# Sparse attention followed by a dense layer: strided loads held behind two DMA transposes, transposes re-ordered, the instruction order dealt anew

## The chip, the cores and the metric

One NeuronCore of a Trainium2 chip runs the whole program. The metric is the device time of one execution in microseconds (us), lower is better. Its engines are TensorE (PE in the profile, PEld for its weight loads), VectorE (DVE), ScalarE (ACT), GpSimd (POOL) and SyncE (SP). Here POOL issues all loads, which turn float32 into bfloat16 on the way, and SP issues all stores of the output and all DMA transposes. Each engine works through its own instructions in the order in which the program gives them.

## The reference

Eight batches of eight heads, 576 positions, head size 64. Heads 0 to 3 attend locally (the last 32 positions), heads 4 to 7 with a stride (positions that are a multiple of 32 back). The result, 4608 tokens of 512 features, goes through a dense layer with an ELU between two matrices.

```python
B, H, S, D = q.shape            # 8, 8, 576, 64
scores = scale * np.matmul(q, k.transpose(0, 1, 3, 2))
rel = pos[:, None] - pos[None, :]
mask_local = (rel >= 0) & (rel < stride)                       # heads 0 to 3
mask_strided = (rel >= 0) & (pos[None, :] % stride == pos[:, None] % stride)   # 4 to 7
attn = softmax(where(mask, scores, -1e9))
x = (attn @ v).transpose(0, 2, 1, 3).reshape(B * S, H * D)     # 4608 x 512
h = x @ w_in                                                   # 512 -> 2048
g = np.where(h > 0.0, h, np.exp(np.minimum(h, 0.0)) - 1.0)
out = g @ w_out                                                # 2048 -> 512, float32
```

## The kernel before

Attention is done batch by batch and the dense layer chunk by chunk, 512 tokens to a chunk, nine chunks. A batch has 576 tokens, so chunk 4 (tokens 2048 to 2559) needs batches 3 and 4, chunk 5 batches 4 and 5, chunk 6 batches 5 and 6. The normalised result of attention is kept transposed in `xT` (features on partitions), the form that the dense layer's matmuls read.

What each engine does, and when, is written out by hand in one list of tokens, `ORDER`. The program goes through it and records the instructions of each token; the queue of each engine is therefore the tokens of that engine in this order, and a token's place among tokens of other engines matters only for what it can depend on. The tokens:

- `4s0.tq@2` and the like belong to attention: batch 4, kind s (strided) or l (local), pair of heads 0 or 1; the number after @ is the PSUM bank, the letter after / the engine (A for ACT, D for DVE, S for a DMA transpose from SP). The steps of a pair: `tq`, `tk`, `cq`, `ck` transpose q and k on TensorE and copy them (batches 0 to 2 only); `S` scores; `e`, `F0`, `F1` the exponentials on ACT; `m0`, `M` the masks on DVE; `v0`, `v1`, `halo` bring v into place; `a` is probabilities times v; `n` normalises into `x_sb` on DVE (the profile's x_s and x_l, L661 and L663).
- Then x has to be transposed into `xT`. Early batches do it on TensorE (`x`, L671) with a copy `y`. From batch 4 on it is done by DMA. For local heads `y/S` is one DMA transpose from SP (L685) straight into `xT`. For strided heads `z` is a DMA transpose from SP (L679) into a part of the tile `qT_str` of that batch, which is free by then, and `y` is a copy by DVE or ACT from there into `xT` (L700, L702).
- `i4.0@2` is hidden tile 0 (of 16) of chunk 4: four matmuls over the four feature blocks (L739), in `C_ORDER`, which takes the strided heads first: 4s0's block, 4s1's, then the local ones. `x4.0@2` is its Exp on ACT (L744). `r4.0` and `g4.0` finish the ELU: `r/D` is L750 on DVE, `r/A` a Relu on ACT (L748), `g` is L759 or L756 on DVE.
- `o4.1.2` is a quarter of the sixteen output matmuls of 128 tokens (L765); `c4.1/A` copies the result out of PSUM (L772) and issues its store from SP (L780). The three buffers `o_sb` are used in turn.
- `load.6` issues all loads of batch 6 from POOL: local q, k, v (L299, L303, L287), then strided q, k, v (L275, L279), each strided tensor as five DMAs. At most eight of POOL's DMAs are under way at a time: each issue waits for the landing of the one eight before it. The same holds for SP's DMAs.
- From batch 3 on, q and k are transposed by DMA: `turn.6s` (L309, two DMA transposes, q then k) and `turn.6l` (L315, four), from SP. Each waits for its loads, and all that follows on SP waits with it.

In the list of before, the queue of SP has between chunks 1 and 5 this order (`c` is a store): `turn.4s turn.4l c1.3 c2.0 turn.5s c2.1 turn.5l 4l0.y c2.2 4l1.y 4s0.z 4s1.z c2.3 turn.6l c3.0 c3.1 turn.6s 5s0.z 5l0.y c3.2 5l1.y 5s1.z c3.3 turn.7l c4.0 turn.7s c4.1 6l0.y 6l1.y c4.2 6s0.z 6s1.z`. POOL has `load.2` to `load.7` one after the other.

Of the kernel before, what the change touches and what calls it, by code (L numbers as in the profile page):

```python
# [11 lines left out]
BF16 = mybir.dt.bfloat16  # L12
# [39 lines left out]
0l0.tq@2 0s1.n@1 0l1.tq@3 0l0.cq/A 0s0.x@4 0l1.cq/A 0l0.s1@0 0s0.y/D load.2 0l1.s0@1  # L52
0l0.e1 0l0.halo/D 0s1.x@2 0l1.e0 0l1.s1@0 0s1.y/D 0l0.s0@1 0l1.e1 0l1.halo/D 0l0.e0
mk.l busy.2 0l1.a@0 0l0.a@1 0l1.n@0 0l0.n@1 busy.2 0l1.x@3 i0.0.0@4 0l1.y/A i0.2.0@2
i0.0.1 0l0.x@0 i0.1.0@3 i0.1.1 0l0.y/D i0.2.1 i0.0.2 i0.0.3 i0.1.2 i0.1.3 x0.0@0
i0.2.2 i0.2.3 x0.1@1 i0.3@5 r0.0/D x0.2@2 g0.0 r0.2/D r0.1/A x0.3@0 g0.1 r0.3/D i0.4@4
# [18 lines left out]
r1.10/A x1.12@2 g1.10 r1.11/A r1.12/D i1.14@2 x1.13@1 g1.11 g1.12 r1.13/A i1.15@5
load.4 x1.14@0 g1.13 o1.0.0@3 r1.14/A x1.15@2 g1.14 o1.0.1 r1.15/D g1.15 2l0.S@0,1,4,2
o1.0.2 2l0.e o1.1.0@5 2l0.F0 2l0.m0 2l0.F1 2l1.e o1.0.3 2l0.M 2l0.a@0 2l1.m0 3s0.v0/A
turn.3s o1.1.1 2l0.n@0 3s0.v1/A 2l1.a@1 c1.0/A o1.1.2 3s1.halo/D 2l1.n@1 2l0.x@4
o1.1.3 turn.3l 2l0.y/D 2l1.x@2 o1.2.0@3 c1.1/A 2l1.y/D i2.0@4 i2.1@5 x2.0@1 i2.2@2
r2.0/D x2.1@0 g2.0 o1.2.1 r2.1/A x2.2@2 g2.1 i2.3@4 r2.2/D i2.4@5 g2.2 x2.3@1 i2.5@2  # L80
r2.3/D x2.4@0 g2.3 o1.2.2 r2.4/A x2.5@2 g2.4 i2.6@4 r2.5/D i2.7@5 g2.5 x2.6@1 i2.8@2
r2.6/D x2.7@0 g2.6 load.5 o1.2.3 r2.7/A x2.8@2 g2.7 i2.9@4 r2.8/D c1.2/A g2.8
3s0.S@0,1,5,3 x2.9@1 i2.10@2 r2.9/D 3s0.e g2.9 3s0.F0 i2.11@4 3s0.m0 3s0.F1 3s1.e
3s0.M 3s0.a@0 x2.10@0 i2.12@5 3s1.m0 x2.11@2 3s0.n@0 turn.4s 3s1.a@1 r2.10/A o1.3.0@3
r2.11/A 3s1.n@1 x2.12@1 3s0.x@0 o1.3.1 3s0.y/A g2.10 3s1.x@1 r2.12/A g2.11 turn.4l
i2.13@2 3s1.y/A g2.12 i2.14@4 x2.13@0 o1.3.2 r2.13/D x2.14@2 g2.13 i2.15@5 r2.14/A
g2.14 o1.3.3 x2.15@1 3l0.S@0,1,2,4 r2.15/D c1.3/A g2.15 o2.0.0@3 3l0.e o2.0.1 3l0.F0
3l0.m0 3l0.F1 3l1.e 3l0.M o2.0.2 3l1.m0 3l0.a@0 o2.0.3 3l0.n@0 3l1.a@1 c2.0/A 3l0.x@5
3l1.n@1 o2.1.0@2 3l0.y/A 3l1.x@4 o2.1.1 3l1.y/D i3.0@3 i3.1@5 x3.0@0 4s0.v0/D i3.2@4
r3.0/D x3.1@2 g3.0 o2.1.2 r3.1/A 4s0.v1/D x3.2@1 g3.1 load.6 i3.3@3 r3.2/D i3.4@5 g3.2  # L90
x3.3@0 turn.5s i3.5@4 r3.3/D x3.4@2 g3.3 o2.1.3 r3.4/A x3.5@1 g3.4 i3.6@3 r3.5/D
c2.1/A g3.5 4l0.S@0,1,5,2 turn.5l x3.6@0 i3.7@4 r3.6/D 4l0.e g3.6 4l0.F0 i3.8@3 4l0.m0
4l0.F1 4l1.e 4l0.M o2.2.0@5 x3.7@2 4l1.m0 i3.9@2 x3.8@1 r3.7/D g3.7 r3.8/A o2.2.1
x3.9@0 g3.8 i3.10@4 r3.9/D g3.9 4s1.halo/A o2.2.2 x3.10@2 4l0.a@0 r3.10/D 4l1.a@1
4l0.n@0 i3.11@3 o2.2.3 4l1.n@1 4l0.y/S x3.11@1 i3.12@2 r3.11/A g3.10 c2.2/A g3.11
x3.12@0 4s0.S@0,1,4,5 4l1.y/S r3.12/D i3.13@3 g3.12 4s0.F0 4s0.F1 4s0.e o2.3.0@4 4s0.M
4s1.e o2.3.1 4s0.m0 x3.13@2 4s0.a@0 4s1.m0 i3.14@5 4s0.n@0 r3.13/A 4s1.a@1 x3.14@1
o2.3.2 4s1.n@1 4s0.z r3.14/A i3.15@2 g3.13 o2.3.3 g3.14 x3.15@0 4s1.z o3.0.0@3 r3.15/D
c2.3/A g3.15 5l0.S@0,1,5,4 o3.0.1 5l1.e o3.0.2 5l0.e 5l1.m0 turn.6l o3.1.0@2 5l0.F0
5l0.m0 5l0.F1 o3.0.3 5l0.M o3.1.1 c3.0/A o3.1.2 4s0.y/A o3.1.3 5s0.v0/D 5s0.S@0,1,5,4  # L100
c3.1/A 4s1.y/D o3.2.0@3 5s0.e 5s0.v1/D turn.6s load.7 i4.0@2 5s0.F0 5s0.m0 5s0.F1
5s1.e i4.1@5 5s0.M x4.0@2 i4.2@4 5s1.m0 x4.1@1 r4.0/D o3.2.1 g4.0 r4.1/A x4.2@0 g4.1
i4.3@2 r4.2/D i4.4@5 g4.2 x4.3@2 i4.5@4 r4.3/D x4.4@1 g4.3 5s0.a@0 r4.4/A i4.6@2
x4.5@0 g4.4 o3.2.2 r4.5/D x4.6@2 g4.5 i4.7@5 r4.6/A 5s0.n@0 5s1.halo/A i4.8@4 g4.6
5s0.z x4.7@1 5l0.a@1 x4.8@0 5l1.a@0 5l0.n@0 i4.9@2 r4.7/A r4.8/A o3.2.3 5l1.n@1
5l0.y/S x4.9@2 5s1.a@1 r4.9/A g4.7 c3.2/A g4.8 i4.10@5 5l1.y/S g4.9 i4.11@3 5s1.n@1
x4.10@1 i4.12@4 r4.10/A x4.11@0 5s1.z g4.10 o3.3.0@2 x4.12@2 r4.11/D i4.13@5 g4.11
r4.12/A g4.12 o3.3.1 x4.13@1 5s0.y/D o3.3.2 r4.13/A g4.13 i4.15@3 o3.3.3 x4.15@0
o4.0.0@4 r4.15/D c3.3/A g4.15 i4.14@5 6l0.S@0,1,2,3 x4.14@2 o4.0.1 r4.14/D 6l0.e g4.14
o4.0.2 6l0.F0 5s1.y/D 6l0.F1 6l1.e o4.0.3 6l0.m0 turn.7l i5.0@5 6l0.M c4.0/A 6l1.m0  # L110
# [44 lines left out]
def kernel(  # L155
# [9 lines left out]
    nc = tc.nc  # L165
# [837 lines left out]
```

## Time and profile before

| | us |
|---|---|
| median of three runs (lowest to highest) | 317.56 (315.15 to 317.68) |
| the profiled execution | 316.84 |
| its span, first to last instruction | 315.0 |
| TensorE busy in it | 299.4 (95%) |
| DVE busy | 216.3 (69%) |
| ACT busy | 194.1 (62%) |

Lines of the profile are read so. In the window view a line is a stretch (from:to, its length), then the busy time and number of instructions of PE, PEld, DVE, ACT and POOL, then the granted TensorE clock (1.00 is full), the mean busy share of the 16 DMA engines, and GB/s. In the timeline a line is the start, the duration (merged over xN instructions), the engine (SPq for what SP's queue issues), the line of the kernel, and in brackets the idle time of the engine before it and what ended that. In the page's groups a line ends with busy time, mean ns of one, and the idle time before. For a DMA, the duration in the timeline is that of its issue; the time to landing stands in views of its own.

### The profile page before, as it was taken

To read this page: it belongs to the slowest core of one execution; us is meant where nothing else is said; L and a number is where in the kernel's file an instruction comes from. 1 tells how busy PE (TensorE), PEld (TensorE's weight loads), DVE (VectorE), ACT (ScalarE), POOL (GpSimd) and SP (SyncE) were. 2 spreads that over 40 slices of the span, in tenths; PEclk is the share of its full clock that TensorE was granted. 3 is DMA by queue.
4 is the path that set the end of the run, shared out by engine and by line. 5 is a ranking of instruction groups with operands and counts; after the bars stand their busy time and mean duration, and the time that the engine had idled before them with its cause. 6 is when DMAs were issued, how large, how long until landed. Compare 5 with 4: busy or idle time off the path is not lost.

```text
span 315.0 us, 6035 instructions
## 1 busy us (share of the span) xinstructions
PE 299.4 (95%) x2227; PEld 156.8 (50%) x2264; DVE 216.3 (69%) x425; ACT 194.1 (62%) x353; POOL 127.5 (40%) x200
## 2 busy tenths in 40 slices
PE   8989999999999999999799999999999999999992
PEld 3644555655554554554345454544554454444440
DVE  4769734799768876896279687985896486666400
ACT  8748636799557856875569586556667554443210
POOL 8845337797694786766356742000000000000000
PEclk9999999999999999999989999999999999999998
DMA  6999999999999999999999999920033301112012
GB/s 102 141 204 210 210 153 212 125 109 100 138 154 161 134 184 151 116 179 152 144 124 186 166 147 150 194 67 33 33 74 75 67 2 34 33 39 66 33 69 73
DMA packets 113348, 37.35 MB, mean 119 GB/s; under 512 B 95848, under 2 KB 107760, under 8 KB 113312
## 3 DMA queue, kind: packets, MB, share of 16 engines
q0 software_dynamic: 71232, 18.41, 69.8%
q1 hardware_dynamic: 42080, 18.49, 34.8%
q8 instruction: 19, 0.31, 0.5%
q14 instruction: 17, 0.14, 0.2%
HBM read 36.70 MB, written 9.44 MB: 146 GB/s over the span
## 4 chain that ended last, share of the span: by engine, by line
PE 77%; DVE 12%; DMA 4%; issue 2%; ACT 2%; POOL 0%; ACTq 0%; DVEq 0%
PE single L765 35%; PE single L739 32%; DMA qT_str<-x_s 3%; DVE g_sb L759 3%; PE pair L651 3%; DVE g_sb L756 2%; DVE g_sb L750 2%; PE single L405 2%; PE pair L558 2%; DVE x_s L663 1%; DVE x_l L663 1%; DMA q_loc<-in_q_dram 1%; PE single L671 1%; ACT pr L636 1%; DVE rden L661 1%
## 5 line engine op out<-in xcount | busy, mean ns | idle before, releaser
L739 PE MATMUL single<-xT,w_in 128*128 128x512 bf16 x559 | 139.3, 383 | 4.8 <-ACT o_sb L772 2.0
L765 PE MATMUL single<-w_out_sb,g_sb 128*128 128x512 bf16 x558 | 136.5, 379 | 1.7 <-issue 0.8
L744 ACT ACTIVATE e_sb<-single 128x512 f32<-128x512 f32 x144 | 86.0, 602 | 66.6 <-PE single L739 63.0
L739 PEld LDWEIGHTS <-w_in 128*128 128x128 bf16 x576 | 64.0, 114 | 61.9 <-issue 7.7
L765 PEld LDWEIGHTS <-g_sb 128*128 128x128 bf16 x576 | 54.4, 98 | 61.8 <-issue 0.5
L750 DVE TENSOR_SCALAR g_sb<-e_sb 128x512 bf16<-128x512 f32 x89 | 40.8, 458 | 38.2 <-ACT e_sb L744 37.9
L759 DVE TENSOR_TENSOR g_sb<-g_sb,single 128x512 bf16<-128x512 bf16 x89 | 61.0, 687 | 3.1
L756 DVE SCALAR_TENSOR_TENSOR g_sb<-e_sb,g_sb 128x512 bf16<-128x512 f32 x55 | 37.1, 688 | 2.4 <-ACT g_sb L748 2.3
L636 ACT ACTIVATE pr<-pair 128x960 bf16<-128x960 f32 (+4 forms) x36 | 32.0, 900 | 7.2 <-PE single L558 4.1
L772 ACT COPY o_sb<-single 128x512 f32<-128x512 f32 x31 | 18.2, 586 | 26.1 <-PE single L765 25.9
L748 ACT ACTIVATE g_sb<-single 128x512 bf16<-128x512 f32 x55 | 32.6, 600 | 0.0
L651 PEld LDWEIGHTS <-pr 128*128 128x128 bf16 (+3 forms) x364 | 15.1, 102 | 5.8 <-DVE pr L611 0.6
L299 POOL DMA_DIRECT2D q_loc<-in_q_dram x20 | 15.3, 794 | 4.6 <-DMA k_str<-in_k_dram 2.7
L299 POOL DMA_DIRECT2D k_loc<-in_k_dram x20 | 15.0, 762 | 3.9 <-DMA v_raw<-in_v_dram 2.1
L663 DVE TENSOR_TENSOR x_l<-pair,rden 96x768 bf16<-96x768 f32 x16 | 15.3, 954 | 0.6
L663 DVE TENSOR_TENSOR x_s<-pair,rden 126x640 bf16<-126x640 f32 (+1 forms) x16 | 14.0, 874 | 0.5
L269 POOL DMA_DIRECT2D v_raw<-in_v_dram x18 | 10.7, 602 | 7.2 <-DMA w_out_sb<-in_moe_w_out_dram 4.8
L275 POOL DMA_DIRECT2D q_str<-in_q_dram x20 | 12.7, 646 | 1.1 <-DMA k_loc<-in_k_dram 1.0
L275 POOL DMA_DIRECT2D k_str<-in_k_dram x20 | 12.2, 621 | 2.0 <-DMA q_str<-in_q_dram 1.4
L275 POOL DMA_DIRECT2D v_raw<-in_v_dram x20 | 12.2, 626 | 1.6 <-DMA k_str<-in_k_dram 0.9
L661 DVE RECIPROCAL rden<-pair 96x12 f32<-96x12 f32 (+4 forms) x48 | 7.8, 189 | 6.8 <-PE pair L651 3.4
L287 POOL DMA_DIRECT2D v_loc<-in_v_dram x9 | 10.8, 1198 | 3.3 <-DMA q_str<-in_q_dram 1.2
(125 smaller groups left out, 226.5 us busy)
## 6 DMA issues: line engine op xcount, KB each, us to landing
out_dram<-o_sb SPq DMA_DIRECT2D x30, 256.0 KB, 4.2
w_in<-in_moe_w_in_dram POOLq DMA_DIRECT2D x4, 512.0 KB, 11.4
w_out_sb<-in_moe_w_out_dram POOLq DMA_DIRECT2D x4, 512.0 KB, 17.8
v_loc<-in_v_dram POOLq DMA_DIRECT2D x7, 288.0 KB, 9.4
out_dram<-o_sb SPq DMA_DIRECT2D x12, 128.0 KB, 2.3
q_str<-in_q_dram POOLq DMA_DIRECT2D x20, 67.5 KB, 8.2
k_str<-in_k_dram POOLq DMA_DIRECT2D x20, 67.5 KB, 7.2
v_raw<-in_v_dram POOLq DMA_DIRECT2D x20, 67.5 KB, 7.4
```

The costliest lines, as they stand in the source:

```text
L275: nc.gpsimd.dma_start(out=t[0:n, h, 0:run].rearrange("p g d -> p (g d)"), in_=rows[h, :, 0:30, :].rearrange("t (a g) d -> a t (g d)", g=run))
L299: nc.gpsimd.dma_start(out=t[:, h // 2, 0:4, h % 2], in_=src[name][b, h, 0:512].rearrange("(i p) d -> p i d", p=128))
L636: nc.scalar.activation(t, sc[0:t.shape[0], :, 0:w], ACT.Exp, scale=scale)
L651: nc.tensor.matmul(av[0:m, p, blk, :], lhsT=self.pr[0:k, o:o + m], rhs=vt[0:k, 2 * self.hp + p, blk, :], start=True, stop=True)
L663: nc.vector.tensor_tensor(self.x[0:nq, 0:n].rearrange("q g p d -> q p g d"), av[0:nq, :, 0:n, 0:D], rd[0:nq, :, 0:n].unsqueeze(3).to_broad ...
L739: nc.tensor.matmul(h_of[c, i], lhsT=w_in_part(w_in_sb, cc, i), rhs=xT[:, cc, c * N_TILE:(c + 1) * N_TILE], start=j == 0, stop=j == KC - 1)
L744: nc.scalar.activation(e_sb[slot], h_of[c, i], ACT.Exp)
L748: nc.scalar.activation(g[:, i, :], h_of[c, i], ACT.Relu)
L750: nc.vector.tensor_scalar(g[:, i, :], e, scalar1=1.0, scalar2=1.0, op0=ALU.min, op1=ALU.subtract)
L756: nc.vector.scalar_tensor_tensor(g[:, i, :], e, 1.0, g[:, i, :], op0=ALU.subtract, op1=ALU.min)
L759: nc.vector.tensor_tensor(g[:, i, :], g[:, i, :], h_of[c, i], op=ALU.max)
L765: nc.tensor.matmul(out_of[c, i], lhsT=g[:, m, i * 128:(i + 1) * 128], rhs=w_out_sb[:, m, :], start=(m == 0), stop=(m == MC - 1))
```

## The change

Three things are edited.

`load_batch` can issue a part of a batch's loads, and a new token `hold` copies one element of the tile that `z` writes, on POOL, so that POOL waits there until that DMA transpose has landed:

```diff
+    held = consts.tile([1, 1], BF16, tag="held")
...
-    def load_batch(b):
-        for load_one in ((load_strided, load_local) if b < E_LOC else
-                         (load_local, load_strided)):
-            for name in "qkv":
-                load_one(b, name)
+    def load_batch(b, first=0, end=6):
+        both = ((load_strided, load_local) if b < E_LOC else (load_local, load_strided))
+        steps = [(load_one, name) for load_one in both for name in "qkv"]
+        for load_one, name in steps[first:end]:
+            load_one(b, name)
...
-                load_batch(int(rest))
+                load_batch(*(int(i) for i in rest.split(".")))
+        elif what == "hold":
+
+            nc.gpsimd.tensor_copy(held, pairs[rest].bank["z"][0:1, 0, 0:1])
```

POOL's tokens become `load.6.0.3` (local q, k, v), `hold.4s1`, `load.6.3.6` (strided q, k, v), `load.7.0.3`, `hold.5s1`, `load.7.3.6`, in place of `load.6 load.7`.

The queue of SP changes in these places (one token to a line, `y` and `z` as above):

```diff
 turn.4s
+c1.3
 turn.4l
-c1.3
 c2.0
+turn.5l
 turn.5s
 c2.1
-turn.5l
 4l0.y
-c2.2
 4l1.y
+c2.2
 4s0.z
 4s1.z
...
 turn.6s
 5s0.z
 5l0.y
-c3.2
 5l1.y
+c3.2
 5s1.z
-c3.3
 turn.7l
+c3.3
 c4.0
-turn.7s
 c4.1
 6l0.y
+turn.7s
 6l1.y
 c4.2
 6s0.z
 6s1.z
```

The rest of `ORDER` is dealt anew in detail: no token of TensorE moves by more than a few places and no bank changes; Relus `r` on DVE go from 89 to 81 (55 to 63 on ACT), copies `c` on DVE from 4 to 11 (32 to 25 on ACT), and some twelve other copies change engine, among them `5s0.y` (DVE to ACT) and `3s1.y` and `6s1.y` (ACT to DVE). Excerpts that the text speaks of (TensorE's tokens are those with i, o, S, a, x and a bank):

```diff
-3l1.n@1 o2.1.0@2 3l0.y/A 3l1.x@4 o2.1.1 3l1.y/D i3.0@3 i3.1@5 x3.0@0 4s0.v0/D i3.2@4
+c2.0/A o2.1.0@2 o2.1.1 3l0.x@5 3l0.y/A 3l1.n@1 3l1.x@4 3l1.y/D i3.0@3 x3.0@0 r3.0/D
...
-c3.1/A 4s1.y/D o3.2.0@3 5s0.e 5s0.v1/D turn.6s load.7 i4.0@2 5s0.F0 5s0.m0 5s0.F1
+o3.1.1 o3.1.2 o3.1.3 c3.0/A 4s0.y/A 5s0.S@0,1,5,4 5s0.F1 5s0.e o3.2.0@3 c3.1/D turn.6s
+5s0.v0/D load.7.0.3 i4.0@2 5l0.M 5s0.F0 5s1.e 5s0.m0 i4.1@5 5s0.M 5s1.m0 x4.0@2 i4.2@4
```

More of the change, by code (lines that the diff above doesn't have):

```diff
@@ L51 @@
 0s1.e0 busy.1 0s1.s1@1 0s0.v0/D 0s0.a@0 0s1.e1 mk.s 0s0.n@0 busy.1 0s1.a@1 busy.1
[L52 to L56, printed above, removed]
@@ L75 @@
[L75 to L80, printed above, removed]
@@ L81 @@
[L81 to L86, printed above, removed]
@@ L142 @@
[L142 to L146 removed]
+0l0.tq@2 0s1.n@1 0l1.tq@3 0l1.cq/D 0l0.cq/A 0s0.x@4 0l0.s1@0 load.2 0l0.e1 0s1.x@2
+0l1.s0@1 0l1.e0 0l1.s1@0 0l1.e1 0s1.y/D 0l0.s0@1 0l1.halo/D 0l0.e0 busy.2 0l0.halo/D
@@ new lines @@
+4s1.e 4s0.M o2.3.0@4 o2.3.1 x3.13@2 r3.13/A 4s0.m0 4s0.a@0 4s1.m0 4s0.n@0 4s1.a@1
+4s1.n@1 i3.15@2 i3.14@5 x3.14@1 r3.14/D g3.14 o2.3.2 o2.3.3 4s0.z x3.15@0 r3.15/A
+4s1.z hold.4s1 load.6.3.6 g3.13 o3.0.0@3 o3.0.1 g3.15 o3.0.2 o3.1.0@2 c2.3/A
+5l0.S@0,1,5,4 5l0.e 4s1.y/D 5l0.F1 5l1.e 5l1.m0 turn.6l 5l0.m0 5s0.v1/D 5l0.F0 o3.0.3
+o3.1.1 o3.1.2 o3.1.3 c3.0/A 4s0.y/A 5s0.S@0,1,5,4 5s0.F1 5s0.e o3.2.0@3 c3.1/D turn.6s
+5s0.v0/D load.7.0.3 i4.0@2 5l0.M 5s0.F0 5s1.e 5s0.m0 i4.1@5 5s0.M 5s1.m0 x4.0@2 i4.2@4
```

162 lines of the change are left out of this document (86 added, 76 removed).

## The prediction

> **What bounds the kernel now.** I read the page first, then busy time by windows, the timeline of TensorE's one gap, and the sync queue in order of time.
>
> ```profile
> span 315.0 us, 6035 instructions
> PE 299.4 (95%) x2227; PEld 156.8 (50%) x2264; DVE 216.3 (69%) x425; ACT 194.1 (62%) x353; POOL 127.5 (40%) x200
> PEclk9999999999999999999989999999999999999998
> ```
>
> ```profile
> 20.00:60.00 40.00, 37.99 (x403) 21.89 (x409) 26.75 (x53) 24.95 (x47) 20.13 (x34) 1.00 1.46 192
> 60.00:100.00 40.00, 38.72 (x304) 21.00 (x308) 33.18 (x62) 29.63 (x56) 30.86 (x46) 1.00 1.53 124
> ...
> 156.30:159.70 3.40, 3.40 (x9) 1.22 (x8) 2.54 (x5) 2.76 (x7) 1.82 (x4) 0.50 1.24 89
> 159.70:163.00 3.30, 3.30 (x17) 1.64 (x16) 2.16 (x5) 1.77 (x5) 1.48 (x3) 1.00 1.63 119
> 200.00:260.00 60.00, 59.63 (x365) 30.52 (x371) 44.51 (x86) 37.22 (x69) 0.00 (x0) 1.00 0.25 65
> 309.50:313.30 3.80, 0.00 (x0) 0.00 (x0) 0.42 (x1) 0.27 (x1) 0.00 (x0) 1.00 0.24 80
> 313.30:315.00 1.70, 0.00 (x0) 0.00 (x0) 0.00 (x0) 0.00 (x0) 0.00 (x0) 0.51 0.02 5
> ```
>
> The reader is to see that TensorE sets the time: from 200 to 260 us it is busy 59.63 of 60. Only what moves its idle time counts. From 20 to 100 us it idles 2.0 + 1.3 = 3.3 us, in pieces. And one slice of the clock line in mid-run is below 9: at 156.3 to 159.7 us the granted clock is 0.50. Just before it is the one large gap:
>
> ```profile
> 141.95 0.82 DVE L663 TENSOR_TENSOR x_s<-pair,rden 126x640 bf16<-126x640 f32 x1
> 142.57 1.52 SPq L685 DMA_TRANSPOSE xT<-x_l  x1
> 143.04 1.24 POOL L275 DMA_DIRECT2D q_str<-in_q_dram  x2
> 144.19 2.88 SPq L679 DMA_TRANSPOSE qT_str<-x_s  x2
> 152.85 0.59 POOL L279 DMA_DIRECT2D k_str<-in_k_dram  x1 [5.17 <-DMA v_loc<-in_v_dram]
> 154.09 1.16 ACT L700 COPY xT<-qT_str 128x540 bf16<-128x540 bf16 x1 [3.77 <-DMA qT_str<-x_s]
> 154.40 0.60 POOL L275 DMA_DIRECT2D k_str<-in_k_dram  x1 [0.16 <-DMA q_str<-in_q_dram]
> 155.25 0.68 DVE L700 COPY xT<-qT_str 128x540 bf16<-128x540 bf16 x1 [6.06 <-DMA qT_str<-x_s]
> 155.92 4.44 PE L739 MATMUL single<-xT,w_in 128*128 128x512 bf16 x12 [2.04 <-ACT o_sb L772]
> ```
>
> Chunk 4's first matmuls (`i4.0`) need batch 4's strided x, both halves. These pass the sync queue as two DMA transposes (`4s0.z`, `4s1.z`, L679, issued from 144.19), then a copy each (`y`, L700). ACT waits 3.77 us and DVE 6.06 us for the transposes; TensorE goes on at 155.92. Its row shows 2.04 us of idle; I take 2.2, since a first matmul slips in before it.
>
> **The change part by part.** *1. Turns of batch 5 change places, so the z get out earlier.* What stands before the z on SP now:
>
> ```profile
> 126.27 1.93 SPq L309 DMA_TRANSPOSE qT_str<-q_str  x1
> ...
> 132.17 4.03 SPq L315 DMA_TRANSPOSE qT_loc<-q_loc  x2
> 136.25 3.44 SPq L315 DMA_TRANSPOSE kT_loc<-k_loc  x2
> ```
>
> `turn.5l` (L315) stands behind `turn.5s` (L309), which waits for its load until 126.27; so it issues from 132.17 to 139.7, and `4l0.y`, the store `c2.2`, `4l1.y` and both z come after it without a pause. Changed, `turn.5l` goes first, into the time SP spends waiting, and SP is free at about 132. Then each z issues when its x is normalised: the second is ready at 141.95 + 0.82 = 142.8, so `4s1.z` issues at 143.1 instead of 145.7. The price is that `c1.3`'s store now precedes `turn.4l` and holds it until that copy is made, some 4 us by my estimate; the scores of 4l come more than a dozen TensorE tokens (of 0.86 us) later.
>
> *2. The strided loads of batch 6 wait for 4s1.z* (`hold.4s1`). How long do transposes take to land? One view of the tile qT_str over three windows (around 145, around 172, after 203 us):
>
> ```profile
> DMA to landing us min/median/max: 9.6/9.7/9.8
> DMA to landing us min/median/max: 7.2/7.3/7.3
> DMA to landing us min/median/max: 2.6/2.6/2.6
> ```
>
> The last is with no loads in flight. With five to seven strided loads fewer in flight, and v_loc's still there, I take 6.5 for the z of batch 4, nearest the middle row: landed at 149.6 (145.7 to 152.8 by the outer rows). With 0.85 us of copy, x is there at 150.5, 3 us before `i4.0` can start. Even at 9.7 us it is 153.7, and the gap shrinks to 0.2 us. **Gain: 2.2 us.**
>
> *3. The half clock goes with the gap.* TensorE stands still for 2 us and the clock is 0.50 for the next 3.4; after the last matmul at 309.5 it falls to half again, 3.8 us into idleness. I read the drop as the gap's consequence: 3.4 x 0.5 = **1.7 us**. The Trainium skill (TensorE: Matmul & The Clock Gate, Part 1) says the clock halves after at least one idle window of about 3.4 us on a free-running grid; a gap of 2 us does not fill one, so by the letter of that rule the drop would have another cause. The trace has the drop 0.4 us after the gap, which fits a window mostly idle. The rival below goes by the letter.
>
> *4. What the held loads make late.* Behind `hold.4s1` on POOL stand ten q and k strided loads, v, all loads of batch 7, and `hold.5s1`. On SP `turn.6s` waits for q and k, and batch 5's z and y stand behind it:
>
> ```profile
> 160.09 4.47 SPq L309 DMA_TRANSPOSE qT_str<-q_str  x1
> 164.78 4.36 SPq L309 DMA_TRANSPOSE kT_str<-k_str  x1
> 169.24 1.45 SPq L679 DMA_TRANSPOSE qT_str<-x_s  x1
> 170.78 1.45 SPq L685 DMA_TRANSPOSE xT<-x_l  x1
> ...
> 174.78 1.22 SPq L679 DMA_TRANSPOSE qT_str<-x_s  x1
> ...
> ```
>
> ```profile
> 182.13 0.66 DVE L700 COPY xT<-qT_str 128x540 bf16<-128x540 bf16 x1 [0.37 <-DMA qT_str<-x_s]
> ```
>
> ```profile
> 183.09 2.11 PE L739 MATMUL single<-xT,w_in 128*128 128x512 bf16 x9
> ```
>
> This is the tight place. `5s1.y` ends at about 182.9 and `i5.0` needs it at 183.1: 0.2 us of slack. With TensorE 3.9 us ahead it is wanted at 179.2. POOL's rows give the delay: the first strided load moves from 143.04 to about 150, but POOL stood 5.17 us in that stretch waiting for v_loc. Ten issues of 0.6 us put k's last at about 156.3, against 154.40. Landing of such loads, median, first in 117 to 127 us with SP nearly silent, then in 143 to 161:
>
> ```profile
> k_str<-in_k_dram POOLq DMA_DIRECT2D x4, 67.5 KB, 5.2
> ...
> k_str<-in_k_dram POOLq DMA_DIRECT2D x4, 67.5 KB, 10.8
> ```
>
> So k lands between 161.5 and 167.1. `turn.6l` now runs during the hold, which leaves the loads more room; I take 163. The second half of `turn.6s` then ends at about 166 instead of 169.1. The 5.5 us from 169.24 to 174.78 stay, so `5s1.z` issues at 171.6 and, with 7.3 to land and 0.75 for the copy, x is there at 179.7. **Loss at `i5.0`: 0.5 us** (0 to 4.6 by the ends).
>
> *5. Batch 7's turns.* `turn.7l` goes ahead of the store `c3.3` and costs that store 10 us, which no one awaits: its buffer is reused by `c4.2`, over 15 us on. `turn.7s` goes between `6l0.y` and `6l1.y`:
>
> ```profile
> 199.50 2.90 SPq L685 DMA_TRANSPOSE xT<-x_l  x2
> ...
> 203.13 3.69 SPq L679 DMA_TRANSPOSE qT_str<-x_s  x2
> ```
>
> ```profile
> 215.32 1.89 PE L739 MATMUL single<-xT,w_in 128*128 128x512 bf16 x8
> ```
>
> Two halves of 1.6 to 2.2 us unloaded (first row of batch 5: 1.93) put 4 us before `6l1.y` and the z; the z had half that from waiting for their x, so they issue some 2 us later, to 209, land 2.6 us after, and chunk 6 starts at 215 (211 moved ahead). Covered, with little left. If SP has no slack there, up to 2 us.
>
> *6. The two hold copies* have one element each. Nearest POOL rows are DMA issues of 0.6 us; between 0.1 and 0.6 us apiece, behind a wait anyway: nothing.
>
> *7. The new deal.* TensorE's order changes by swaps of neighbours. Of 144 Relus, 89 stood on DVE and 81 do now; 4 stores' copies were on DVE and 11 are now.
>
> ```profile
> L750 DVE TENSOR_SCALAR g_sb<-e_sb 128x512 bf16<-128x512 f32 x89 | 40.8, 458 | 38.2 <-ACT e_sb L744 37.9
> L748 ACT ACTIVATE g_sb<-single 128x512 bf16<-128x512 f32 x55 | 32.6, 600 | 0.0
> L772 ACT COPY o_sb<-single 128x512 f32<-128x512 f32 x31 | 18.2, 586 | 26.1 <-PE single L765 25.9
> ```
>
> ACT takes 8 x 0.60 and gives 7 x 0.59: +0.7 us; DVE gives 8 x 0.46 and takes 7 copies at about 0.7: +1.2. Neither is near full (69% and 62%). Single spots: `i3.0` now follows `3l1.x` directly, without the 0.86 us token that hid a 0.44 to 0.66 us copy; chunk 0 starts its first Exp earlier and waits longer for `0l0.y`. Bounds: at best the 3.3 us idle between 20 and 100, at worst a wait of 0.3 to 0.5 in each of eight chunks, 4 us. I take **+0.4**.
>
> **Sum.** The profiled execution took 316.84 us: its span and 1.8 around it. 316.84 - 2.2 - 1.7 + 0.5 + 0.4 = **313.8**. The three runs shown have a median of 317.56, 0.7 above it; measured from there the sum would be 314.5.
>
> **The rivals.**
> *Clock drop of its own:* the half clock comes at that time whatever TensorE did. 313.8 + 1.7 = 315.5. For it: only 2 of the 3.4 us before were idle. Against: no other drop while matmuls run.
> *Second wait takes the gain:* `5s1.z` lands no earlier than now; TensorE then waits 3.7 us at `i5.0` and probably loses 1.7 to the clock there: 316.9 to 318.6. For it: 0.2 us of slack. Against: `turn.6s` was late for its data, which get more room.
> *The hold does not help:* the z land when they did, the clock falls again: 317.
> *Slower, the hold starves batch 6's chain:* the DMA rate, not the order, sets landing. The z take 9.7 us (152.8), k's last load issues at 159.4 and takes 10.8: 170.2. `turn.6s` is then 5.6 us later than now, batch 5's x comes at 188.5, and TensorE, 3.9 us ahead, waits 3.7 + 5.6 at `i5.0` and loses 1.7 to the clock: 316.84 - 3.9 + 9.3 + 1.7 = 323.9. It decides from where k lands after about 164. For it: DMA share is above 1.4 throughout. Against: POOL's 5.17 us wait is part of the hold.
> *The deal costs cover* in every chunk: 316.84 - 3.9 + 8 = 321.
>
> **How the numbers follow.** Forecast 0.55 (own range 312.2 to 315.3), clock 0.08, second wait 0.11, no help 0.05, starved 0.15, deal 0.06. A measurement of this kernel can tell about 1% from no change: below 314.4 is faster, above 320.7 slower. Faster: 0.45 of the forecast. Same: the forecast's other 0.10, clock, no help, most of the second wait, a third of the deal: 0.35. Slower: starved, most of the deal, the rest: 0.20. The range 312.0 to 318.8 holds all but the two slow cases.
>
> **What would show it.** Right: the z (L680 there) around 143 land within 8 us, no TensorE idle piece over 1 us after 100 us, PEclk 9 at 156, and `turn.6s` ended before 168. Wrong: a half clock anywhere before 309 us; DVE or ACT waiting over 1 us for qT_str while TensorE stands at L740 (the old L739); SP sitting at L310 (the old L309) past 168.

## The result, and the profile after

| | before | after |
|---|---|---|
| median of 22 runs each, us | 317.62 (313.84 to 322.15) | 313.58 (312.49 to 317.27) |
| ratio of after to before | | 0.9899, 95% interval 0.9876 to 0.9921 |
| the profiled execution, us | 316.84 | 313.04 |
| its span | 315.0 | 311.3 |

The change makes the kernel 1.0% faster; the interval excludes no change, and the gain is small. Medians here and below are of all runs shown; ratios leave out runs more than 1.5% above the fastest of their kernel.

The page of the changed kernel, the same lines as before:

```profile
span 311.3 us, 6024 instructions
PE 297.0 (95%) x2227; PEld 156.1 (50%) x2264; DVE 216.1 (69%) x423; ACT 193.2 (62%) x355; POOL 129.3 (42%) x202
PEclk9999999999999999999999999999999999999998
```

The clock line has its only 8 at the end, after the last matmul. The windows, with the stretch around the old gap cut in three:

```profile
20.00:60.00 40.00, 38.20 (x401) 21.79 (x408) 28.39 (x55) 24.47 (x46) 20.45 (x34) 1.00 1.45 191
60.00:100.00 40.00, 38.08 (x286) 20.49 (x289) 32.61 (x60) 29.02 (x56) 33.88 (x50) 1.00 1.46 128
149.00:152.40 3.40, 3.35 (x17) 1.39 (x18) 1.52 (x4) 3.38 (x6) 3.40 (x6) 1.00 1.68 187
152.40:155.80 3.40, 3.40 (x34) 1.93 (x34) 2.63 (x6) 3.12 (x7) 1.93 (x4) 1.00 1.40 165
155.80:159.20 3.40, 3.35 (x25) 1.88 (x25) 3.03 (x7) 2.18 (x4) 2.09 (x4) 1.00 1.34 153
200.00:260.00 60.00, 59.63 (x356) 30.38 (x362) 44.02 (x85) 36.05 (x66) 0.00 (x0) 1.00 0.26 64
```

TensorE is busy through 149 to 159 us, the clock at 1.00. The timeline shows why:

```profile
139.57 0.53 SPq L781 DMA_DIRECT2D out_dram<-o_sb  x1
142.26 2.52 SPq L680 DMA_TRANSPOSE qT_str<-x_s  x2
...
148.28 0.65 DVE L701 COPY xT<-qT_str 128x540 bf16<-128x540 bf16 x1 [2.16 <-DMA qT_str<-x_s]
148.31 0.68 POOL L837 COPY held<-qT_str 1x1 bf16<-1x1 bf16 x1 [3.31 <-DMA qT_str<-x_s]
148.93 1.25 POOL L276 DMA_DIRECT2D q_str<-in_q_dram  x2
...
151.46 1.18 ACT L701 COPY xT<-qT_str 128x540 bf16<-128x540 bf16 x1
153.87 2.75 PE L740 MATMUL single<-xT,w_in 128*128 128x512 bf16 x11
```

POOL stands in the hold until 148.3, and only then issues batch 6's strided loads. The z have landed by then. ACT's copy carries no wait: it is behind other ACT work, not behind the transpose. `i4.0` starts on the heels of `o3.2.0`, with no idle time before it. The time from issue to landing of the tile qT_str, in the windows 141 to 146, 162 to 172 and 200 to 212 us (batches 4, 5, 6):

```profile
DMA to landing us min/median/max: 4.7/5.0/5.2
DMA to landing us min/median/max: 6.3/6.6/6.9
DMA to landing us min/median/max: 2.6/2.6/2.6
```

They were 9.7, 7.3 and 2.6.

### The profile page after: what moved, and what is told of

The parts are those of the page before. It is cut to its first block, busy times and chain, and to the rows that moved or that the text cites. A ratio compares the mean times of both kernels' runs of the same rounds, so it can differ in the third digit from the quotient of the medians.

```text
span 311.3 us, 6024 instructions
## 1 busy us (share of the span) xinstructions
PE 297.0 (95%) x2227; PEld 156.1 (50%) x2264; DVE 216.1 (69%) x423; ACT 193.2 (62%) x355; POOL 129.3 (42%) x202
## 4 chain that ended last, share of the span: by engine, by line
PE 80%; DVE 14%; ACT 2%; issue 2%; DVEq 0%; ACTq 0%
PE single L766 37%; PE single L740 32%; DVE g_sb L760 3%; PE pair L652 3%; DVE g_sb L751 3%; DVE g_sb L757 2%; PE pair L559 2%; DVE x_s L664 2%; PE single L406 1%; ACT e_sb L745 1%; DVE x_l L664 1%; ACT pr L637 1%; DVE rden L662 1%; PE single L453 1%; PE single L559 1%
## 5 line engine op out<-in xcount | busy, mean ns | idle before, releaser
L740 PE MATMUL single<-xT,w_in 128*128 128x512 bf16 x562 | 136.4, 379 | 3.8 <-DVE g_sb L760 2.4
L766 PE MATMUL single<-w_out_sb,g_sb 128*128 128x512 bf16 x555 | 134.2, 379 | 1.8 <-issue 0.8
L760 DVE TENSOR_TENSOR g_sb<-g_sb,single 128x512 bf16<-128x512 bf16 x81 | 55.6, 687 | 2.7
L757 DVE SCALAR_TENSOR_TENSOR g_sb<-e_sb,g_sb 128x512 bf16<-128x512 f32 x63 | 42.8, 688 | 20.0 <-ACT g_sb L749 19.8
L751 DVE TENSOR_SCALAR g_sb<-e_sb 128x512 bf16<-128x512 f32 x81 | 37.0, 456 | 28.2 <-ACT e_sb L745 27.9
L749 ACT ACTIVATE g_sb<-single 128x512 bf16<-128x512 f32 x63 | 37.5, 601 | 0.0
L773 ACT COPY o_sb<-single 128x512 f32<-128x512 f32 x25 | 14.8, 592 | 17.2 <-PE single L766 16.9
L270 POOL DMA_DIRECT2D v_raw<-in_v_dram x18 | 10.8, 610 | 7.8 <-DMA w_out_sb<-in_moe_w_out_dram 4.9
L773 DVE COPY o_sb<-single 128x512 f32<-128x512 f32 x10 | 6.9, 688 | 10.2 <-PE single L766 9.3
```

The source lines that it names most:

```text
L740: nc.tensor.matmul(h_of[c, i], lhsT=w_in_part(w_in_sb, cc, i), rhs=xT[:, cc, c * N_TILE:(c + 1) * N_TILE], start=j == 0, stop=j == KC - 1)
L749: nc.scalar.activation(g[:, i, :], h_of[c, i], ACT.Relu)
L751: nc.vector.tensor_scalar(g[:, i, :], e, scalar1=1.0, scalar2=1.0, op0=ALU.min, op1=ALU.subtract)
L757: nc.vector.scalar_tensor_tensor(g[:, i, :], e, 1.0, g[:, i, :], op0=ALU.subtract, op1=ALU.min)
L760: nc.vector.tensor_tensor(g[:, i, :], g[:, i, :], h_of[c, i], op=ALU.max)
L766: nc.tensor.matmul(out_of[c, i], lhsT=g[:, m, i * 128:(i + 1) * 128], rhs=w_out_sb[:, m, :], start=(m == 0), stop=(m == MC - 1))
```

## The experiments

Twelve runs followed, one of them the kernel before once more. Nine are timed, each beside the kernel before on the same chip; the other three (`before_again`, `gaps`, `gaps_25`) are one profiled execution each. The diffs show tokens of `ORDER`, cut at `...`.

**The queue's order alone** (the tokens of SP between 3l and 4s0.z).

```diff
-turn.4l c1.3 c2.0 turn.5s c2.1 turn.5l 4l0.y c2.2 4l1.y
+c1.3 turn.4l c2.0 turn.5l turn.5s c2.1 4l0.y 4l1.y c2.2
```

> The kernel before with only the sync queue's order changed (local turns of batch 4 after c1.3's copy, local turns of batch 5 ahead of its strided ones, 4l1.y ahead of the store c2.2); strided loads not held, old deal. Theory (both parts are needed): the second z of batch 4 issues at 143 instead of 145.7 us, still lands some 9.7 us later because the loads of batch 6 are in flight, x comes at 153.7 and the gap at i4.0 is 0 to 0.5 us with the clock at 1.0; but batch 6's strided turns and so the second z of batch 5 are no earlier than before, so TensorE, 3.5 us ahead, waits about 3 us at i5.0: ratio 0.995 to 1.000, 316 to 317.6. Rival (the queue order alone does it): no wait at i5.0 either, ratio 0.989, 314. Rival (the order does nothing, the DMA rate sets the landing): z land near 155 as before, gap and half clock stay, 1.000.

Measured: 314.43, ratio 0.9905 (0.9869 to 0.9941). No gap at `i4.0`, 0.28 us at `i5.0`. So the theory as I had put it fell: no wait of some 3 us came at `i5.0`, and the order alone brings the gain. But the trace shows that it also held the loads, without a hold. On POOL:

```profile
147.68 1.20 POOL L285 DMA_DIRECT2D v_loc<-in_v_dram  x1 [1.07 <-PE single L763]
148.87 1.25 POOL L273 DMA_DIRECT2D q_str<-in_q_dram  x2
```

The z were issued at 144.9 and 146.3, later than in the kernel before; the first strided load followed at 148.87 instead of 143.04. `turn.5l` now runs while batch 5's strided loads are in flight, the last of these lands at 137.9 instead of 129.7, and since POOL waits for the landing of its eighth DMA back, all its later loads slip.

**The holds alone.**

```diff
-load.6                        ... turn.6s load.7
+load.6.0.3                    ... turn.6s load.7.0.3
+4s1.z hold.4s1 load.6.3.6     ... 5s1.z hold.5s1 load.7.3.6
```

> The kernel before with only the strided loads of batches 6 and 7 held behind 4s1.z and 5s1.z; old order on the sync queue, old deal. Theory (both parts are needed): the second z issues at 145.7 us as before but lands in 5 to 6.5 us, so x comes at 151.6 to 153 and the gap at i4.0 closes, clock 1.0; the strided loads start 2 us later than in the changed kernel, batch 6's strided turns end at 166 to 168, and i5.0 waits 0.5 to 2 us: ratio 0.989 to 0.994, 314.2 to 315.8. Rival (the queue order is what counts): z land after 154, gap of 1 us or more left, ratio 0.996 to 1.0. Rival (a hold starves batch 6's chain when it stands alone): i5.0 waits over 4 us, ratio above 1.003.

Measured: 313.79, ratio 0.9897 (0.9859 to 0.9935); no gap over 0.2 us after 130 us. Landing of the z, here:

```profile
DMA to landing us min/median/max: 5.3/5.7/6.0
```

The wait of 0.5 to 2 us that I had expected at `i5.0` did not come. So each half alone gives all of the gain, as far as intervals of some 0.4% to either side can tell.

**Both, with the old deal and batch 7's turns at their old places.**

> Queue order and holds together on the kernel before, with its old deal and batch 7's turns at their old places. Theory: as the changed kernel without what its new deal costs, 0.4 us by the sum of the prediction and 1.0 us by the profile after, so ratio 0.985 to 0.988, 312.6 to 313.2 where the changed kernel has 313.6; the late turns of batch 7 are covered and their old places cost nothing. Rival (the deal gave part of the gain): ratio above 0.990. Rival (old places of batch 7's turns block the sync queue, since their loads are now held to 191 us): TensorE waits at i6.0 or earlier for 6l or 6s, ratio above 0.992.

Measured: 313.36, ratio 0.9880 (0.9844 to 0.9916), against 313.58 and 0.9899 for the changed kernel: the new deal and the later turns of batch 7 are worth nothing that shows. `turn.7s` ran from 187.8 to 191.9, and no matmul waited for it.

**The gap filled.** Ten matmuls of zeros, added to `o3.2`'s sum, in the gap of the kernel before:

```diff
-o3.2.0@3
+o3.2.0@3 fill.10
```

> The kernel before with ten 128x512 matmuls of zeros, 2.2 us, put between o3.2.0 and i4.0: they add nothing to the output, and they fill the gap in which TensorE waits for batch 4's x. Theory (the half clock is the gap's consequence): i4.0 starts when it did, the clock stays 1.0, and 1.7 us are gained: ratio 0.9946, 315.9. Rival (clock drop of its own): the granted clock is 0.50 around 156 to 160 us as before, ratio 1.000. If the filling itself delayed i4.0, it would start after 156.5, and the ratio would be above by that. The Trainium skill (TensorE: Matmul & The Clock Gate, Part 1) asks for a whole idle window of about 3.4 us before the clock halves; by that the 2 us gap filled here is not the cause and the time stays.

Measured: 317.0, ratio 0.9967 (0.9925 to 1.0008). That cannot tell 0.9946 from 1. The granted clock was 0.996 to 0.999 in all nine runs that the ratio keeps, but 0.990 in two of the three that it leaves out, so this run does not settle what the gap costs. The profiled execution took 320.86 us and is not in the ratio; in it the z were issued 2 to 3 us later than before, and `i4.0` started at 158.5. It holds one fact: a gap of 1.90 us before `i5.0` with no half clock behind it. So a gap does not always cost the clock, which set off the next question.

**The kernel before, profiled once more.**

> The kernel before, unchanged, profiled once more. Theory: the gap at i4.0 is there in every execution (1.5 to 3 us, the z landing 9 to 10 us after their issue), the half clock behind it only in some: of the 17 runs timed with the first experiments 7 show a mean granted clock of 0.986 to 0.992, 10 of 0.994 to 0.999. Rival (the half clock always follows the gap): PEclk shows a slice below 9 again right behind it.

Measured: 319.26 us. The gap at `i4.0` is 1.15 + 0.39 us, and the clock stays full there. But there is a second gap, which the first profile did not have:

```profile
154.84 0.38 PE L739 MATMUL single<-xT,w_in 128*128 128x512 bf16 x1 [1.15 <-ACT o_sb L772]
155.60 2.54 PE L739 MATMUL single<-xT,w_in 128*128 128x512 bf16 x11 [0.39 <-DVE xT L702]
...
177.65 0.65 DVE L700 COPY xT<-qT_str 128x540 bf16<-128x540 bf16 x1 [4.39 <-DMA qT_str<-x_s]
...
180.10 0.20 PE L558 MATMUL single<-qT_loc,kT_loc 64*128 64x96 bf16 x1 [2.23 <-DVE g_sb L759]
```

DVE waits 4.39 us in `5s0.y` for batch 5's first z. Chunk 4's last results (`g4.13`, `g4.15`) stand behind it on DVE, their banks stay full, and the scores `6l0.S` wait 2.23 us for a bank. The half clock now comes there, in windows of 3.41 us:

```profile
177.66:181.07 3.41, 1.18 (x27) 0.82 (x27) 3.34 (x7) 1.12 (x2) 2.35 (x4) 1.00 1.93 206
181.07:184.48 3.41, 3.41 (x10) 1.22 (x8) 1.34 (x5) 1.76 (x4) 0.83 (x2) 0.50 1.79 171
```

The part of my expectation on how often the clock falls can be counted. Of 52 timed runs of the kernel before that the comparisons keep, 14 have a mean granted clock of 0.986 to 0.992 and a median of 318.4 us; 37 have 0.994 or more, and 316.5. The 1.9 us between them is about one half-clock window. (Of all 62 timed runs 23 have 0.985 to 0.992, so the share depends on which runs are kept.) No run of `sp_only`, `hold_only`, `old_deal`, `hold4` or `no_hold` is below 0.994.

**Nine inserted gaps of four lengths.** In chunks 7 and 8 of the kernel with both parts and the old deal:

```diff
-i7.9@2
+i7.9@2 stall.1.7.9.6.2   # DVE: result * 0, then 1 copy; PE: one matmul of it, added to o6.2
```

> Queue order and holds with the old deal, and nine waits of TensorE put into chunks 7 and 8, where the DMA engines are quiet: after an i step, DVE multiplies its result by zero and copies the zeros 1, 3, 5 or 9 times, and TensorE waits for that with one matmul of zeros, which adds nothing. Expected gaps of about 1.3, 2, 2.7 and 4 us, some 20 us in all, 333 us. Theory (the clock is halved for one window of 3.4 us behind a window on a fixed grid in which TensorE was mostly idle, as the profile before has it: 2 us idle, then 0.50 for 3.4 us): behind the 4 us gaps always, behind 2.7 us often, behind 2 us at times, behind 1.3 us never. Rival (a gap of 2 us never halves it, and the drop in the profile before had another cause): only the 4 us gaps show it. The Trainium skill (TensorE: Matmul & The Clock Gate, Part 1) asks for a whole idle window of about 3.4 us; by that only the gaps over 3.4 us can halve it, and those of 4 us only where they cover a whole window of the grid.

Measured: gaps of 0.85, 1.50, 2.16 and 3.47 us. The clock fell behind one of the two 3.47 us gaps, and behind no other. In windows of 3.41 us counted from that drop:

```profile
273.48:276.89 3.41, 0.53 (x3) 0.04 (x1) 2.57 (x9) 0.60 (x1) 0.00 (x0) 1.00 0.27 58
276.89:280.30 3.41, 2.82 (x7) 1.03 (x8) 2.54 (x6) 0.00 (x0) 0.00 (x0) 0.50 0.00 0
...
300.78:304.19 3.41, 1.62 (x8) 0.60 (x6) 1.60 (x5) 1.19 (x2) 0.00 (x0) 1.00 0.00 0
304.19:307.60 3.41, 1.72 (x8) 0.86 (x9) 3.18 (x9) 0.43 (x1) 0.00 (x0) 1.00 0.00 0
```

The first gap lies nearly whole in one window, which has 0.53 us of matmuls: half clock. The second, as long, is cut by a boundary, 1.62 and 1.72 us of matmuls on its sides: full clock. My expectation that a 4 us gap always costs the clock was wrong.

**Nine gaps of 2.5 us.** As above with six copies each.

> As the run with nine inserted gaps, but all of them with six copies, 2.5 us each (estimated from the measured 0.85, 1.50, 2.16 and 3.47 us for one, three, five and nine copies). In the runs so far the clock was 0.50 in the 3.41 us behind windows of 3.41 us in which TensorE was busy for 0.53, 1.18 and 1.32 us, and full behind windows with 1.62, 1.62 and 1.72 us; the windows follow each other without a break, counted from any drop of the run. Theory (the clock halves behind a window with less than some 40 to 47 per cent of busy time): every gap that leaves a window less than 1.3 us of matmuls is followed by a half clock, none that leaves more than 1.6, so 2 to 5 of the nine. Rival (only a window wholly idle counts): none of nine. Rival (any gap over 2 us): all nine.

Measured: nine gaps of 2.49 us, six half-clock windows. Three of the nine, with the window that holds most of the gap and the one after it:

```profile
250.47:253.88 3.41, 0.92 (x5) 0.30 (x4) 2.42 (x9) 0.60 (x1) 0.00 (x0) 1.00 0.00 0
253.88:257.30 3.42, 3.42 (x9) 1.24 (x10) 1.92 (x4) 0.00 (x0) 0.00 (x0) 0.50 0.01 2
...
277.78:281.19 3.41, 1.56 (x8) 0.78 (x9) 3.17 (x10) 0.51 (x1) 0.00 (x0) 1.00 0.00 0
281.19:284.60 3.41, 2.28 (x11) 0.92 (x9) 1.51 (x4) 1.17 (x2) 0.00 (x0) 1.00 0.00 0
...
301.67:305.08 3.41, 1.10 (x6) 0.53 (x7) 3.17 (x10) 0.60 (x1) 0.00 (x0) 1.00 0.07 14
305.08:308.50 3.42, 3.42 (x10) 1.22 (x9) 0.92 (x2) 0.60 (x1) 0.00 (x0) 0.50 0.00 0
```

The six drops follow windows with 0.92 to 1.10 us of matmuls; the three gaps that left 1.56 us or more on each side had none. Both rivals fall (none of nine, nine of nine), and the count is one above my two to five. The gap of `filled` fits: a boundary cut it, with 2.25 and 2.68 us of matmuls on its two sides.

**The strided loads put back ahead of the z**, in the kernel with the queue's order alone:

```diff
-load.6
+load.6.3.6 load.6.0.3
```

> The kernel with only the sync queue's new order, in which the strided loads of batch 6 were issued only from 148.9 us without any hold, after the z had been issued at 144.9 and 146.3; here batch 6's strided loads go ahead of its local ones, so that they are in flight again when the z are issued. Theory (the z land fast only where no strided loads are in flight, whatever keeps these back): the strided loads are issued by 146 us, the z take 8 us or more instead of 4.7 to 6.7, x comes at 153 or later, and a gap of 0.3 to 2 us stands at i4.0 again: ratio 0.993 to 0.998, 315.2 to 316.8. Rival (the earlier issue of the z is what counts): no gap over 0.3 us at i4.0, ratio 0.989 to 0.991 as with the order alone. The local turns of batch 6 then wait for later local loads; if that delays 5s1.z, the loss would stand at i5.0 and not at i4.0.

Measured: 322.76. Five of the six runs lie too far above the sixth for a ratio; the profiled one, of 322.42, is the typical one. The z took 7.8 to 8.3 us again, as expected. But they were issued at 141.7 and 143.0, so their x came in time, and no gap stood at `i4.0`: that part was wrong. The price stood elsewhere:

```profile
169.33 1.43 POOL L273 DMA_DIRECT2D q_str<-in_q_dram  x2
169.70 1.24 SPq L677 DMA_TRANSPOSE qT_str<-x_s  x1
...
180.79 0.65 DVE L698 COPY xT<-qT_str 128x540 bf16<-128x540 bf16 x1 [9.48 <-DMA qT_str<-x_s]
183.25 0.23 PE L556 MATMUL single<-qT_loc,kT_loc 64*128 64x96 bf16 x1 [7.33 <-DVE g_sb L757]
```

Batch 6's local loads came last, and `turn.6l` went out 6 us later than in the kernel before. But `turn.6s` ended at 169.6, 0.5 us later than there, and batch 5's first z was issued 0.5 us later. What was late is its landing: it took 11.0 us, where it had taken 7.2. Batch 7's strided loads went out from 169.3, the first of them ahead of it; in the kernel before they went out from 176.6, when that z had landed. The second tight place then cost 7.33 us and two windows of half clock (179.64 to 186.47). So, by this one profile, the z of batch 5 paid the price that the z of batch 4 pays in the kernel before. The prediction's slower rival has another chain, in which late k loads make `turn.6s` late by 5.6 us.

**The first hold alone.**

> The kernel before with the first hold alone (batch 6's strided loads behind 4s1.z); batch 7's loads, the queue's order and the deal as before. Theory (loads in flight make the z slow, at two tight places): the z of batch 4 land 5 to 6 us after their issue and the gap at i4.0 is gone; batch 6's strided turns end by 167, so batch 5's first z lands by 173 and DVE does not stand in its y; the second z lands with batch 7's strided loads in flight, some 7.3 us, so i5.0 waits 0 to 1 us: ratio 0.989 to 0.993, 314 to 315.4. Rival (both holds are needed): a gap of 2 us or more moves to 6l0.S or i5.0, ratio 0.995 to 1.0.

Measured: 313.97, all six runs in 313.2 to 314.9; ratio 0.9897 (0.9834 to 0.9961). No gap over 0.2 us at `i4.0`, `6l0.S` or `i5.0`. The z were issued at 144.8 and 146.1, no earlier than before, and landed by 152.9, 7.6 and 6.8 us after their issue, slower than the 5 to 6 expected. With both holds the ratio is the same 0.9897, so the second hold adds nothing that shows.

**The second hold alone.**

> The kernel before with the second hold alone (batch 7's strided loads behind 5s1.z). Theory: the gap at i4.0 stays at 1.5 to 2.2 us, in some executions with the half clock behind it; batch 5's second z lands in 5 to 6 us instead of 7.3 to 8.8, but its first z is as late as before and DVE stands in its y for 1 to 4 us: ratio 0.996 to 1.000, 316.2 to 317.6. Rival (the second hold carries the gain): ratio below 0.993.

Measured: 318.40 beside 318.16 for the kernel before; ratio 0.9936 (0.9863 to 1.0010), which rests on four of its twelve runs; no gain is shown. In its profile the z of batch 4 were issued at 143.2 and 144.8, about 1 us earlier than in the kernel before and 1 us later than in the changed one, and took as long to land as before:

```profile
DMA to landing us min/median/max: 9.5/9.6/9.7
```

The gap at `i4.0` was 0.77 us, less than the 1.5 to 2.2 expected, and batch 5's second z took 7.5 us, not the 5 to 6 expected.

**The second tight place by itself.** In the kernel before:

```diff
-x4.13@1 5s0.y/D o3.3.2
+x4.13@1 o3.3.2
-r4.14/D 6l0.e g4.14
+r4.14/D 6l0.e g4.14 5s0.y/D
```

> The kernel before with one token moved: 5s0.y, the copies on DVE that wait for batch 5's first z, goes from ahead of g4.13 to behind g4.14, so that DVE does not hold up chunk 4's last results, whose banks 6l0.S needs. Theory (a second tight place of the kernel before, seen in its second profile as 4.4 us of DVE waiting and 2.2 us of TensorE idle at 6l0.S, with the half clock there): no gap at 6l0.S in any execution, the gap at i4.0 as before; the median gains what that place costs on average, 0.5 to 1.5 us, ratio 0.995 to 0.999. Rival (the place is harmless, the second profile was a disturbed execution): ratio 1.000. If 5s1.y then comes later because 5s0.y runs just before it, i5.0 loses up to 0.9 us.

Measured: 317.84 beside 318.16; ratio 0.9993 (0.9940 to 1.0045). There is no gap at `6l0.S`, and in its place

```profile
156.52 2.98 PE L737 MATMUL single<-xT,w_in 128*128 128x512 bf16 x12 [1.83 <-ACT o_sb L770]
185.21 4.26 PE L737 MATMUL single<-xT,w_in 128*128 128x512 bf16 x19 [2.08 <-DVE xT L700]
```

a gap of 2.08 us at `i5.0`: the second z had been issued at 174.9 and landed at 184.4. The clock stayed at 1.00: a boundary cut that gap, with 1.52 us of matmuls in the window of 3.41 us that holds most of it. Where the wait is taken can be moved; that batch 5's x is late cannot, by this.

**The changed kernel without its holds** (`load.6` and `load.7` whole again, everything else kept).

> The changed kernel without its two holds: batch 6's and batch 7's loads each in one piece, at the places where the local halves stand; new queue order and new deal kept. Theory (any order that gets the strided loads of batch 6 issued after batch 4's z does the work, and the new queue order delays the loads that stand before them): the strided loads are issued after 147 us without a hold, the z land within 7 us, no gap at i4.0; batch 7's strided loads go out about 3 to 10 us earlier than with the hold and slow 5s1.z by 1 to 2 us, so at most 0.5 us at i5.0: ratio 0.989 to 0.992, 314 to 315. Rival (the new deal, with batch 5's loads earlier, lets the strided loads go out before the z): z take 8 us or more, gap back at i4.0 or i5.0, ratio 0.995 to 1.000.

Measured: 314.74, ratio 0.9890 (0.9841 to 0.9938), where the changed kernel has 0.9899: no loss shows in the ratio. Strided loads from 147.2 us on, z landed in 4.6 to 5.3 us, nothing at `i4.0`, and 1.28 us at `6l0.S`. The z behave as expected, and the gap stands at `6l0.S`, not at `i5.0`. There the late landing is that of batch 5's first z, 8.4 us after its issue, where it took 6.3 in the changed kernel.

Issue and landing by the trace, in us, each from one profile:

| kernel | second z of batch 4: issued, landed | first strided load of batch 6 issued | last k landed | second z of batch 5 landed | gaps at i4.0; 6l0.S; i5.0 |
|---|---|---|---|---|---|
| before | 145.7, 155.2 | 143.0 | 164.2 | 182.1 | 2.04; 0; 0 |
| before, again | 144.9, 154.8 | 142.6 | 164.1 | 183.2 | 1.54; 2.23; 0 |
| second hold alone | 144.8, 154.2 | 142.0 | 160.9 | 180.7 | 0.77; 0; 0.29 |
| order alone | 146.3, 151.6 | 148.9 | 165.9 | 181.8 | 0; 0; 0.28 |
| first hold alone | 146.1, 152.9 | 153.6 | 165.0 | 178.9 | 0; 0; 0 |
| both holds | 144.6, 149.9 | 150.6 | 161.5 | 176.7 | 0; 0; 0 |
| after | 143.6, 148.3 | 148.9 | 161.9 | 176.1 | 0; 0; 0 |
| after, no holds | 144.6, 149.2 | 147.2 | 164.8 | 180.8 | 0; 1.28; 0 |
| order and both holds, old deal | 144.2, 150.6 | 151.2 | 163.7 | 178.3 | 0; 0; 0 |
| order, strided loads first (`sp_early`) | 143.0, 151.3 | 132.4 | 147.4 | 187.5 | 0; 7.33; 0 |
| second place by itself (`y_late`) | 146.5, 156.0 | 142.1 | 162.6 | 184.4 | 1.83; 0; 2.08 |

Wherever the first strided load goes out after the second z, that z lands in 4.6 to 6.8 us; where it goes out before, in 9.5 to 9.9 (8.5 in the profile of `filled`), and with the ten q and k loads issued ahead of it (`sp_early`) in 8.3. In `sp_early` neither `turn.6l` (from 154.4) nor `v_loc` (from 157.6) was under way then, so a z can be slow without these two. `v_loc` was under way beside the quick z of both holds and of the changed kernel. How much each of the other loads adds is not shown.

## Why the prediction was right, point by point

It gave 313.8; the profiled execution took 313.04 and the median is 313.58. The main part holds: with the strided loads held the z land soon, and the gap and its half clock go. That the total fits so well is partly luck, as the points below show: terms too large and terms left out cancel.

*1, z issued earlier.* Measured 143.6, predicted 143.1. But the gain does not need it: with the first hold alone the second z went out at 146.1, later than before, and the gap was gone; with the second hold alone it went out at 144.8, 0.9 us earlier than before, landed 9.5 us later, and 0.77 us of the gap was left. An issue at 143.0 is early enough even for a landing in 8.3 us (`sp_early`), so the earlier issue would help where the loads were not held. What the order did by itself was to delay the loads. SP was not free at 132 either: `turn.5s` ran until 135.5 behind late loads, and two transposes of batch 4's local x and the store until 140, harmlessly.

*2, z land in 6.5 us, gain 2.2.* Measured 5.0, and the gap is gone. The mechanism stands, and so does the gain of 2.2 us for this pair.

*3, the half clock goes with the gap, 1.7.* Right for the pair of profiled executions, and the rival of a drop of its own is out: inserted gaps bring the drop, in chunks where there had been none. That the one profile of before had the half clock is luck: it is a chance, 14 of 52 runs, some 0.5 us on average. The reading that the drop fits "a window mostly idle" was right. The Trainium skill (TensorE: Matmul & The Clock Gate, Part 1) has the window's length and that it runs free; its "≥1 idle window" is not what the traces show: 1.32 us of matmuls in a window of 3.41 did not keep the clock up.

```profile
152.91:156.32 3.41, 1.32 (x5) 0.57 (x7) 1.04 (x3) 2.23 (x4) 2.50 (x5) 1.00 1.68 200
156.32:159.73 3.41, 3.41 (x9) 1.22 (x8) 2.56 (x5) 2.77 (x7) 1.83 (x4) 0.50 1.20 89
```

That is the kernel before, at the drop of the prediction, cut at the window's boundaries.

*4, held loads, loss 0.5 at `i5.0`.* Measured none. In the changed kernel's timeline:

```profile
162.02 1.58 SPq L310 DMA_TRANSPOSE kT_str<-k_str  x1
163.71 1.55 SPq L680 DMA_TRANSPOSE qT_str<-x_s  x1
...
169.13 1.28 SPq L680 DMA_TRANSPOSE qT_str<-x_s  x1
...
178.78 0.65 DVE L701 COPY xT<-qT_str 128x540 bf16<-128x540 bf16 x1
179.36 4.48 PE L740 MATMUL single<-xT,w_in 128*128 128x512 bf16 x20
```

`turn.6s` ended at 163.6, not 166; the second z went out at 169.1, not 171.6, and landed at 176.1; its copy was no longer waiting for it. The term that was mis-sized is the end of `turn.6s`. The last k landed at 161.9, where 163 was taken, and the second half then took 1.58 us to issue, where 163 to 166 leaves 3 (it took 4.36 in the kernel before). The prediction shows 10.8 us for the landing of the four large k loads issued from 143 to 161 us in the kernel before, and kept it as its slow end. The same row of the changed kernel, then of the kernel with the holds alone:

```profile
k_str<-in_k_dram POOLq DMA_DIRECT2D x4, 67.5 KB, 7.6
...
k_str<-in_k_dram POOLq DMA_DIRECT2D x4, 67.5 KB, 5.6
```

The prediction had `i5.0` as the tight place. It missed that batch 5's late first z can already cost the kernel before time, at `6l0.S`: in its second profile it does, 2.23 us. Of the six profiles with the first hold five have no gap there, and one (`gaps`) has 0.78 us. So the holds relieve two places, and the sum has only one of them.

On average over the runs the sum is right by cancelling: it counts the half clock in full, 1.7 where some 0.5 is the average, takes 0.5 for a loss at `i5.0` that did not come, and leaves out the second place. In the two profiles of before the gaps are 2.04 and 3.77 us, 2.9 on average; with 0.5 for the clock that is an estimate of 3.4. By the ratio the gain is 3.2 us; the sum has 3.0. (The medians of all runs lie 4.0 apart, those of the runs that the ratio keeps 3.5.)

*5, batch 7's turns.* Covered, as predicted; the z were not even late:

```profile
197.15 1.25 SPq L310 DMA_TRANSPOSE qT_str<-q_str  x1
198.62 1.44 SPq L310 DMA_TRANSPOSE kT_str<-k_str  x1
200.15 1.35 SPq L686 DMA_TRANSPOSE xT<-x_l  x1
...
202.22 2.56 SPq L680 DMA_TRANSPOSE qT_str<-x_s  x2
```

The halves took 1.25 and 1.44 us, less than the 1.6 to 2.2 assumed, and the z went out at 202.2, where they had at 203.1.

*6, hold copies.* 0.68 us for the first, a little above the bound of 0.6, and 0.18 for the second; no gap follows.

*7, the deal, +0.4.* In the pair it is met: TensorE's idle time from 20 to 100 us is 1.80 + 1.92 = 3.72, against 3.29. But eight profiles with the old deal have 2.4 to 5.9 there, 3.55 on average. The term cannot be told from nothing. (By the two lists eight other copies change engine, not some twelve, and `7l1.y` also goes ahead of `c5.2`.)

*The rivals.* The clock drop of its own and the second wait did not come; the hold helps; no chain starved under the holds, and in none of the kernels with the first hold did batch 6's last k land more than 0.8 us later than before; the deal costs no cover that shows.

## What to carry to other kernels

When a small DMA transpose on the path is slow to land, look first at what else is in flight at its issue: holding back the strided loads, which nobody needs yet, took it from 9.7 to 5 us, and the last of k still landed 2.3 us sooner than before (161.9 against 164.2). One hold was enough here: the second hold, the new order and the new deal add nothing that shows on top of it. A place that shows no idle time in one profile can be the one that breaks in the next; take a second profile of the kernel before, and count the granted clock over all runs, before you price a gap. A gap's price in clock depends on where it falls on the window, so price it by its chance.

## What the runs showed of the hardware

- The granted clock halves for a window of 3.41 us behind a window of 3.41 us in which TensorE was little busy. Busy times of 0.53, 0.92 to 1.10, 1.18 and 1.32 us were followed by 0.50; 1.52, 1.56, 1.62 and more by 1.00. All fourteen traces agree, each cut from 12 us on by the boundaries that its last drop gives: no window with 1.32 us or less kept the clock up, none with 1.52 or more lost it. Boundaries run through the whole execution without regard to the work: in `gaps` the clock falls at 276.89 and again after the last matmul near 331.5, 16 windows of 3.413 us later.
- Strided loads and DMA transposes that are in flight together take longer. A z took 9.4 to 9.9 us to land with strided loads issued ahead of it (`before`, `before_again`, the second hold alone), 4.6 to 7.6 where they came after both z, and 2.6 with no loads in flight.
- The loads are slower there too. In the kernel before batch 6's four large k loads took 10.8 us (median) beside `turn.6l`, whose four transposes took 8.7 to 12.1; in the changed kernel 7.6 and 6.2 to 8.3, with the holds alone 5.6 and 2.7 to 6.1. In `hold_only` the first strided load went out 7.6 us later than before and the last k landed 2.7 us earlier (161.5 against 164.2); in `hold4` it went out 10.6 us later and the last k landed 0.8 us later (165.0). What in the chip makes them slow, and which of the two slows the other there, no run here tells.
